# The first unit's x and f_logit loaded by rows and transposed on TensorE, with two more edits at the start of a float32 scan and two-MLP kernel

## The chip, the core and the metric

One Trainium2 chip, one of its cores. The metric is the device time of one execution in microseconds (us); lower is better. The engines are TensorE (PE; PEld is its weight load), VectorE (DVE), ScalarE (ACT), GpSimd (POOL) and SyncE (SP), whose queue issues nearly all transfers.

## The reference

`x` and `f_logit` are (2, 6080, 256), the weights are drawn as float64 and used as two int32 words each (low, high).

```
sig = 1 / (1 + exp(-f_logit)); f = lower_bound + (1 - lower_bound) * sig
h = f[:, t] * h + (1 - f[:, t]) * x[:, t]; y[:, t] = h      # gated scan over t, from h = 0
z = square(relu(y @ w_in1)) @ w_out1                        # 256 -> 2048 -> 256, 12160 tokens
out = elu(z @ w_in2) @ w_out2                               # 256 -> 2048 -> 256
```

## The kernel before

The 12160 tokens are cut into 12 units: the first has two halves of 512 and 384 tokens, all others two halves of 512. Everything on the chip is held with the model dimension on the partitions, as two blocks of 128 (index `c`), and tokens along the row. Float32 products are made of three fp32r matmuls (high by high, high by low, low by high), so each weight and each activation is split into a high part (a copy on ACT or DVE) and a low part (a subtraction on DVE).

The scan is made in four chunks a unit (two for each half). For a chunk `add_scan` issues: loads of f_logit (`fs`) and x (`xs`) on SP, in four transfers each; tanh on ACT (L573); two DVE transposes, `xT` and `fT` (L578; 32 by 32 blocks); for the first chunk the bounds `ga`, `gb` (L588, L589); two gates (L584); the feed `xT = (fT - 1) * xT` (L592); two scans, one for each block `c` (L605); and a copy of the last column to `carry` (L610). A half's parts `xa` or `xb` follow: high on ACT (L485), low on DVE (L488).

The first two units of the first MLP are "plain": for a group `g` of 256 hidden units the PE makes two PSUM tiles (`c0`, `c1`, then `c2`, `c3`) of six matmuls each (L636), ACT takes relu (L728) and square (L661) and the high part `g` (L676), DVE the low part (L681), and the PE then adds `g` by the output weights `wo` into `a00` to `a11` (L858). Units from the third on, and the whole second MLP, use a form with seven weight sums and fewer matmuls.

Weights are prepared on the chip while the first units run: a load `st` (L316 for `w_in1`, L308 for `w_out1`), two ACT steps (L372 for the magnitude, L375 for the low bits), two DVE steps (L378, L381), then the high part on ACT (L407) and the low part on DVE (L413). The first of them is loaded by ACT's queue, the others by SP's. There are three `st` buffers.

The order on each engine is made once, ahead of the run, by `Order.run`: a list scheduler with planned costs (`act(n)`, `dve(n)`, `ROW` us for each column of a matmul) that takes on each engine the ready step with the earliest due time. On the chip each engine then works its list in that order and waits at each instruction for what it needs. DVE and ACT therefore hold up all that stands behind a waiting instruction. A step with an alternative (`("ACT", ...)`) goes to the engine that the planner finds free first.

Of the kernel before, what the change touches and what calls it, by code (L numbers as in the profile page):

```python
# [6 lines left out]

F32 = mybir.dt.float32
# [15 lines left out]
ROW = 1 / 2240  # L24
# [4 lines left out]
    "fs": 2, "xs": 2, "fT": 1, "xT": 1, "F0": 1, "F1": 1, "xa": 1, "xb": 1, "ws": 2, "wp": 2, "r": 3, "e": 2,  # L29
# [122 lines left out]
def kernel(  # L152
# [31 lines left out]
    warm = const.tile([P, 1], F32, name="warm")  # L184
    const.tile([P, GAP], F32, name="gap")
# [20 lines left out]
    def plain(m, u):  # L206
        return m == 0 and u < PLAIN

    def halves(m, u):
        return units[u] if plain(m, u) else (sum(units[u]) // 2,) * 2  # L210
# [85 lines left out]
    def key_of(tag):  # L296
        count[tag] = count.get(tag, -1) + 1
        return tag, count[tag]
# [5 lines left out]
    def load_w(queue, st, m, kind, c):  # L304
        w = ((w_in1, w_out1), (w_in2, w_out2))[m][kind].bitcast(I32)
        if kind == 1:
            v = w[c * CF : (c + 1) * CF, :].rearrange("(k p) u -> p k u", p=P)
            queue.dma_start(st.rearrange("p k e w -> p k (e w)"), v)  # L308
        elif m == 1:
            v = w[:, 2 * c * CF : 2 * (c + 1) * CF].rearrange("(k p) u -> p k u", p=P)  # L310
            queue.dma_start(st.rearrange("p k e w -> p k (e w)"), v)
        else:

            v = w[:, 2 * c * CF : 2 * (c + 1) * CF].rearrange("(q k i) u -> q i k u", q=4, k=KD)
            for q in range(4):
                queue.dma_start(st[32 * q : 32 * q + 32].rearrange("p k e w -> p k (e w)"), v[q])  # L316
# [37 lines left out]
    def add_weights(i, m, kind, c, due, wk=None):  # L354
        t = {}

        def load(e):
            t["st"] = new("st", [P, 2, CE // 2, 2], I32)
            if i == 0:
                nc.scalar.activation(warm, warm, AF.Exp)  # L360
            load_w(nc.scalar if i == 0 else nc.sync, t["st"], m, kind, c)
            if i == 0:
                for k in range(KD):
                    nc.scalar.dma_start(lb[:, k : k + 1], lower_bound.rearrange("(q c i o) -> c q i o", q=4, c=KD, o=1)[k])
            sv = t["st"].rearrange("p k e w -> p (k e) w")
            t["low"], t["high"] = sv[:, :, 0], sv[:, :, 1]
# [51 lines left out]
        def keep_whole(e):  # L418
# [4 lines left out]
            ["ACT" if i == 0 else "SP", 5.8 if i == 0 else 1.9 if m == 0 and kind == 0 else 0.475, load, (), [st], None, 512],  # L423
# [5 lines left out]
        if i == 0:  # L429
            steps[0][4].append(("lb",))  # L430
            order.add(*steps[0][:2], -20.0, *steps[0][2:])
            del steps[0]
# [58 lines left out]

    def add_parts(m, u, F, due, later):

        ns = halves(m, u)
        if plain(m, u):
            for h, n in enumerate(ns):
                tag = ("xa", "xb")[h]
                k = key_of(tag)
                x_k[m, u, h] = [(*k, 0), (*k, 1)]
                def dst(h=h, tag=tag, n=n):  # L500
                    if (m, u, h) not in x_t:
                        x_t[m, u, h] = new(tag, [P, 2, 3 + h, HN], F32R)[:, :, :2, :n]
                    return x_t[m, u, h]
                def src(h=h, n=n):
                    return F_t[m, u][:, h : h + 3 : 2, :n]
                high, low = split(src, dst)
                chain(in_due[m, u, h, 0], [
                    ["ACT", act(2 * n), high, F[h], [x_k[m, u, h][0]]],
                    ["DVE", dve(2 * n), low, [x_k[m, u, h][0], *F[h]], [x_k[m, u, h][1]]],
                ])  # L510
            return
        n = ns[0]
# [43 lines left out]

    def add_scan(i, u, h, q, due, after=None):
        nh = units[u][h]
        n = nh // 2
        t0 = starts[u] + sum(units[u][:h]) + q * n  # L560
        at = q * n
        t = {}

        def load(x, src):
            def go(e):
                t[x] = new(x, [P, CN // 32, KD, 32])[:, : n // 32]
                v = src[t0 : t0 + n, :].rearrange("(n j) (q u) -> q j n u", j=32, q=4)
                for q in range(4):
                    nc.sync.dma_start(t[x][32 * q : 32 * q + 32].rearrange("j n c i -> j n (c i)"), v[q])  # L569
            return go  # L570
# [3 lines left out]

        def turn(src, dst):
            def go(e):
                t[dst] = new(dst, [P, KD, CN])[:, :, :n]
                nc.vector.transpose(t[dst].rearrange("p c (n i) -> p n c i", i=32), t[src])  # L578
            return go
# [29 lines left out]
        def carry_on(e):  # L609
# [5 lines left out]
        opened = [("F0", u, 0, 0)] * (h + q > 0)  # L615
        chain(due, [
# [5 lines left out]
            *([["DVE", 0.2, bound, [("lb",)], [("bound",)]]] if i == 0 else []),  # L622
            *(["DVE", dve(n, True), gate(c), [("bound",)], [fT]] for c in range(KD)),
            ["DVE", dve(N), feed, [fT], [xT]],
            *(["DVE", dve(n) + 0.1, scan(c), [fT, xT, ("carry",), *opened], [F]] for c in range(KD)),
# [80 lines left out]
    def add_plain(s, wk):  # L706
# [24 lines left out]
        for c in range(2):  # L731
            k = order.add("PE", 6 * ROW * n, in_due[s] + 6 * c * ROW * n, product(c), [*x_k[m, u, h], wk], [ck[c], ("pe",)])
            if c == 0:
                n_first[s] = k
# [227 lines left out]
    n_scan = 0  # L962
    for kind, s in pe_order:
        if kind == "out":
            add_out(s)
            continue
        m, u, h, g = s
        if kind != "later" and s == first_of[m, u]:
            if m == 0:
                keys = {}  # L970
                before = slots_of(0, u - 1)
                for hh in range(2):
                    due = in_due[(m, u, hh, 0) if plain(m, u) else s]
                    for q in range(2):
                        k = before[SCANS[2 * hh + q] * len(before) // KG] if u >= BEHIND else None
                        keys[hh, q] = add_scan(n_scan, u, hh, q, due - 6.0 + 2.0 * (q - 1), n_first[k] if k else None)
                        n_scan += 1
                if plain(m, u):
                    add_parts(m, u, [[keys[hh, 0], keys[hh, 1]] for hh in range(2)], None, None)
                else:  # L980
                    f0, f1 = ([keys[hh, 0], keys[hh, 1]] for hh in range(2))
                    add_parts(m, u, (f0, f0, f1, f1), in_due[s], mid_due[s])
            else:
                add_parts(m, u, add_reload(u, in_due[s]), in_due[s], mid_due[s])
        if kind == "plain":
            add_plain(s, use[s])
        elif kind == "first":
            add_first(s, use[s])
        else:
            add_later(s)  # L990

    with tc.manual_schedule():
        nc.vector.memset(warm, 0.0)
        order.run()
# [25 lines left out]
```

## Time and profile before

| | |
|---|---|
| time of the runs | 2000.31 us median (2000.08, 2000.31, 2001.04) |
| profiled execution | 2000.24 us, span of the trace 1998.4 us |
| PE busy | 1963.1 us (98%) |
| DVE busy | 1674.6 us (84%) |
| ACT busy | 1633.3 us (82%) |
| first matmul starts | 19.61 us |

The execution's own time is 1.84 us more than the span of its trace. A matmul of 512 columns takes 0.227 us where twelve run back to back at full clock (2.72 us for twelve). An engine's column "idle before" names what ended the wait. "SPq" and "ACTq" are transfers being issued by those engines.

### The profile page before, as it was taken

The page shows a single profiled execution, that of the slowest core. Times are in us where ns is not written, and L with a number is a line of the kernel's source. Part 1 is how long each engine was busy: PE and PEld are TensorE (multiplying, and loading weights), DVE is VectorE, ACT ScalarE, POOL GpSimd, SP SyncE. Part 2 cuts the span into 40 slices and gives each one's busy share as a digit, 9 for nine tenths or more (in the row PEclk, how much of TensorE's full clock was granted, in tenths as well). Part 3 has the DMA queues.
Part 4 walks back from the last instruction along what each step waited for, and adds up shares of the span by engine and source line. Part 5 has one row for each costly group of instructions (what it writes and reads, how often), then busy time and mean ns, then how long its engine had stood idle before and what let it go on. Part 6 is the DMA issues. An engine that isn't in the chain of part 4 may idle for free.

```text
span 1998.4 us, 24516 instructions
## 1 busy us (share of the span) xinstructions
PE 1963.1 (98%) x8688; PEld 1628.9 (82%) x8688; DVE 1674.6 (84%) x2291; ACT 1633.3 (82%) x2164; POOL 0.2 (0%) x4
## 2 busy tenths in 40 slices
PE   5999999999999999999999999999999999999998
PEld 4987888888888888888888888888888888888886
DVE  7879998887987987888898798798888887779886
ACT  6988988888888888878888888887887888788885
POOL 0000000000000000000000000000000000000000
PEclk9999999999999999999999999999999999999999
DMA  7877762433443344244243344334324323334231
GB/s 196 244 226 229 263 207 93 143 129 108 125 127 113 126 122 134 96 148 139 86 136 122 113 135 127 121 111 137 129 83 132 134 93 113 114 113 135 87 106 53
DMA packets 235138, 267.30 MB, mean 134 GB/s; under 512 B 160008, under 2 KB 160776, under 8 KB 235016
## 3 DMA queue, kind: packets, MB, share of 16 engines
q1 hardware_dynamic: 234432, 265.21, 41.6%
q8 instruction: 68, 1.11, 0.2%
q10 hardware_dynamic: 584, 0.53, 0.1%
q14 instruction: 54, 0.44, 0.1%
HBM read 221.91 MB, written 43.78 MB: 133 GB/s over the span
## 4 chain that ended last, share of the span: by engine, by line
PE 91%; DVE 5%; DMA 1%; ACT 1%; issue 1%; SPq 1%; DVEq 0%; ACTq 0%
PE a L858 48%; PE c L636 43%; DVE g L681 1%; DVE a L342 1%; SPq L569 0%; DMA fs<-in_f_logit_dram 0%; DMA a<-rd 0%; DMA xs<-in_x_dram 0%; ACT g L676 0%; DMA st<-in_moe_w_in_dram 0%; DVE a L378 0%; DVE a L381 0%; DVE fT L578 0%; DVE F L605 0%; DVE s L763 0%
## 5 line engine op out<-in xcount | busy, mean ns | idle before, releaser
L858 PE MATMUL a<-g,wo 128*128 128x512 f32 (+1 forms) x4608 | 1099.0, 387 | 1.2 <-DVE g L681 1.0
L858 PEld LDWEIGHTS a<-g,wo 128*128 128x128 f32 x4608 | 863.3, 188 | 175.5 <-DVE g L681 3.1
L681 DVE TENSOR_TENSOR g<-r,g 128x1024 fp32r<-128x1024 f32 (+2 forms) x384 | 463.0, 1206 | 153.6 <-ACT g L676 152.0
L636 PE MATMUL c<-xb,ws 128*128 128x512 f32 (+2 forms) x2208 | 525.9, 387 | 0.0
L636 PEld LDWEIGHTS c<-xb,ws 128*128 128x128 f32 x2208 | 414.0, 188 | 82.4
L676 ACT ACTIVATE g<-r 128x1024 fp32r<-128x1024 f32 (+2 forms) x384 | 403.6, 1051 | 94.1 <-PE a L858 82.8
L636 PE MATMUL c<-xa,ws 128*128 128x512 f32 (+1 forms) x1680 | 417.7, 392 | 27.1 <-ACT xa L485 19.6
L636 PEld LDWEIGHTS c<-xa,ws 128*128 128x128 f32 x1680 | 316.4, 189 | 98.2 <-ACT xa L485 19.6
L759 ACT ACTIVATE s<-c 128x512 f32<-128x512 f32 (+1 forms) x528 | 307.5, 588 | 14.1 <-PE c L636 13.5
L671 DVE SCALAR_TENSOR_TENSOR r<-e,r 128x1024 f32<-128x1024 f32 (+1 forms) x192 | 232.1, 1209 | 29.9 <-ACT e L668 29.9
L665 ACT ACTIVATE e<-r 128x1024 f32<-128x1024 f32 (+1 forms) x192 | 201.7, 1051 | 48.7 <-DVE r L803 48.3
L661 ACT ACTIVATE r<-r 128x1024 f32<-128x1024 f32 x192 | 201.8, 1051 | 2.4
L668 ACT ACTIVATE e<-e 128x1024 f32<-128x1024 f32 (+1 forms) x192 | 201.7, 1050 | 1.6
L763 DVE TENSOR_TENSOR s<-s 128x512 f32<-128x512 f32 (+1 forms) x176 | 119.9, 681 | 74.5 <-ACT s L759 74.5
L799 ACT ACTIVATE r<-c 128x512 f32<-128x512 f32 (+1 forms) x176 | 104.2, 592 | 82.6 <-PE c L636 82.1
L796 DVE TENSOR_TENSOR s<-c,s 128x512 f32<-128x512 f32 (+1 forms) x176 | 120.3, 684 | 20.3 <-PE c L636 18.0
L807 DVE TENSOR_TENSOR r<-c,s 128x512 f32<-128x512 f32 (+1 forms) x176 | 119.3, 678 | 4.5 <-DVE g L681 0.5
L803 DVE TENSOR_TENSOR r<-c,s 128x512 f32<-128x512 f32 (+1 forms) x176 | 119.6, 680 | 2.1
L810 DVE TENSOR_TENSOR r<-s 128x512 f32<-128x512 f32 (+1 forms) x176 | 119.1, 677 | 0.0
L655 ACT ACTIVATE r<-r 128x1024 f32<-128x1024 f32 x80 | 84.4, 1055 | 3.3 <-DVE r L810 3.3
L658 ACT ACTIVATE r<-r 128x512 f32<-128x512 f32 x80 | 50.4, 630 | 33.7 <-DVE r L803 33.0
L605 DVE TENSOR_TENSOR_SCAN F<-fT,carry,xT 128x256 f32<-128x256 f32 (+2 forms) x94 | 65.4, 723 | 1.1
(47 smaller groups left out, 757.2 us busy)
## 6 DMA issues: line engine op xcount, KB each, us to landing
ws<-wd SPq DMA_DIRECT2D x176, 896.0 KB, 4.9
fs<-in_f_logit_dram SPq DMA_DIRECT2D x184, 64.0 KB, 2.2
xs<-in_x_dram SPq DMA_DIRECT2D x184, 64.0 KB, 2.2
xd<-o SPq DMA_DIRECT2D x46, 256.0 KB, 4.5
F<-xd SPq DMA_DIRECT2D x22, 512.0 KB, 4.5
out_dram<-o SPq DMA_DIRECT2D x88, 128.0 KB, 2.3
st<-in_moe_w_out_dram SPq DMA_DIRECT2D x16, 512.0 KB, 5.2
wd<-wp SPq DMA_DIRECT2D x24, 256.0 KB, 3.7
```

The source lines that it names most:

```text
L636: nc.tensor.matmul(out, lhsT=ws[:, p, w], rhs=xs[:, r, v], start=start and q == 0, stop=stop and q == 2, skip_group_check=check,)
L661: nc.scalar.activation(r_t[0], r_t[0], AF.Square)
L665: nc.scalar.activation(t["e"], r_t[0], AF.Relu, scale=-1.0)
L668: nc.scalar.activation(t["e"], t["e"], AF.Exp, scale=-1.0)
L671: nc.vector.scalar_tensor_tensor(r_t[0], t["e"], 1.0, r_t[0], op0=ALU.subtract, op1=ALU.max)
L676: nc.scalar.activation(g_t[s, which][:, 0], r_t[0], AF.Copy)
L681: nc.vector.tensor_tensor(g_t[s, which][:, 1], r_t[0], g_t[s, which][:, 0].bitcast(F32), op=ALU.subtract)
L759: nc.scalar.activation(t["s"][:, c - 1], t[c], AF.Copy)
L763: nc.vector.tensor_tensor(t["s"][:, 1], t["s"][:, 1], t["s"][:, 2], op=ALU.add)
L796: nc.vector.tensor_tensor(t["s"][:, 0], t[0], t["s"][:, 0], op=ALU.add)
L803: nc.vector.tensor_tensor(odd[0][:, 1], t[2], t["s"][:, 0], op=ALU.add)
L858: nc.tensor.matmul(a, lhsT=y, rhs=v, start=begin and jj == 0 and p == 0, stop=end and jj == len(mine) - 1 and p == 2, skip_group_check=True,)
```

## The change

Five things are edited.

1. `w_in1`'s rows and all scan channels are paired: partition p holds model dimensions 2p and 2p + 1 rather than one from each of two 32-blocks. A load of `w_in1` and of `lower_bound` is then one transfer each instead of four and two, and the DVE transposes of later units read their source at a step of two elements.
2. For the first unit `fs` and `xs` are loaded by rows (tokens on the partitions, one transfer each), and the PE transposes them into PSUM against an identity `one`; tanh and the feed read PSUM. The identity is made on GpSimd by `make_identity`. The unit's chunks are cut at multiples of 128 tokens: 256, 256, 256 and 128 (before: 256, 256, 192, 192).
3. The first half's parts are made for each block `c` apart, high and low, and the first group's products are ordered by block: six matmuls that need only block 0, then six for block 1.
4. `fT` has two buffers; the second half's scans are entered in the order after the first half's.
5. The planner's costs: `ROW` from 1/2240 to 1/2258, a gate at `dve(n)`, a scan at `0.1 + n / 490`, one load of `w_in1` at 0.475.

```diff
-ROW = 1 / 2240
+ROW = 1 / 2258
-    ... "fT": 1, ...
+    ... "fT": 2, ...
@@ load_w
-            v = w[:, 2 * c * CF : 2 * (c + 1) * CF].rearrange("(q k i) u -> q i k u", q=4, k=KD)
-            for q in range(4):
-                queue.dma_start(st[32 * q : 32 * q + 32].rearrange("p k e w -> p k (e w)"), v[q])
+            v = w[:, 2 * c * CF : 2 * (c + 1) * CF].rearrange("(p k) u -> p k u", k=KD)
+            queue.dma_start(st.rearrange("p k e w -> p k (e w)"), v)
+    def add_first_parts(F, k, src, dst, n, due):
+        x_k[0, 0, 0] = [(*k, c, p) for c in range(KD) for p in range(2)]
+        cut = [split(lambda c=c: src()[:, c], lambda c=c: dst()[:, :, c]) for c in range(KD)]
+        for c, (high, low) in enumerate(cut):
+            f = [(*v, c) for v in F]
+            hi, lo = (*k, c, 0), (*k, c, 1)
+            order.add("ACT", act(n), due - 3.0, high, f + [(*k, 0, 0)] * c, [hi])
+            order.add("DVE", dve(n), due - 2.0, low, [hi, *f], [lo])
@@ add_scan
+        def load_rows(x, src):
+            def go(e):
+                t[x] = new(x, [P, CN // 32, 32, KD]).rearrange("p n i c -> p (n i c)")[:, : n * KD].rearrange("p (k d) -> p k d", d=D)
+                nc.sync.dma_start(t[x], src[t0 : t0 + n, :].rearrange("(k p) d -> p k d", p=P))
+            return go
+        def turn_rows(x, tag):
+            def go(e):
+                out = pools[tag].tile([P, HN], F32, tag=tag, name=tag)
+                t[tag] = out.rearrange("p (c n) -> p c n", c=KD)[:, :, :n]
+                v = t[x].rearrange("p k (i c) -> p k c i", c=KD)
+                for k in range(n // P):
+                    for c in range(KD):
+                        nc.tensor.transpose(t[tag][:, c, k * P : (k + 1) * P], v[:, k, c], one)
+            return go
-                nc.vector.transpose(t[dst].rearrange("p c (n i) -> p n c i", i=32), t[src])
+                nc.vector.transpose(t[dst].rearrange("p c (n i) -> p n c i", i=32), t[src].rearrange("p n i c -> p n c i"))
+        if u == 0:
+            tags = [("c0", "c1"), ("c2", "c3"), ("a10", "a11"), ("a00", "a01")][i]
+            pf, px = (key_of(tag) for tag in tags)
+            order.add("SP", 0.6, -20.0 + 2 * i, load_rows("fs", ff), (), [fs], None, n)
+            order.add("SP", 0.6, -19.0 + 2 * i, load_rows("xs", xf), (), [xs], None, n)
+            if i == 0:
+                order.add("SP", 0.6, -18.5, load_bound, (), [("lb",)])
+            order.add("PE", 0.1 * n / P * KD, due - 6.0, turn_rows("fs", tags[0]), [fs, ("one",)], [pf, ("pe",)])
+            order.add("PE", 0.1 * n / P * KD, due - 6.0, turn_rows("xs", tags[1]), [xs], [px, ("pe",)])
+            chain(due, [
+                ["ACT", act(N, True), tanh_turned(tags[0]), [pf], [fT]],
+                *([["DVE", 0.2, bound, [("lb",)], [("bound",)]]] if i == 0 else []),
+                *(["DVE", dve(n), gate(c), [("bound",)], [fT]] for c in range(KD)),
+                ["DVE", dve(N), feed_turned(tags[1]), [px, fT], [xT]],
+                *(["DVE", 0.1 + n / 490, scan(c), [fT, xT, ("carry",), *opened], [F, (*F, c)]] for c in range(KD)),
+                ["DVE", 0.1, carry_on, [F], [("carry",)]],
+            ])
+            return F
@@ add_plain
+        if n_plain[0] == 1:
+            for k in range(2):
+                x_k1 = x_k[m, u, h][2 * k : 2 * k + 2]
+                n1 = order.add("PE", 6 * ROW * n, in_due[s] + 6 * k * ROW * n, products_of(k), [*x_k1, wk], [ck[0], ck[1], ("pe",)])
@@ end
         nc.vector.memset(warm, 0.0)
+        make_identity(nc, one)
         order.run()
```

On the PE the list of matmuls is otherwise the same from end to end; what is new stands at its start. Before, the first rows of PE are these (`xa` is the first half's parts, `ws` and `s` are weights):

```order
L636 MATMUL c0_290<-xa_272,ws_249 128x512 x6
L636 MATMUL c1_305<-xa_272,ws_249 128x512 x6
L636 MATMUL c2_334<-xa_272,s_317 128x512 x6
L636 MATMUL c3_348<-xa_272,s_317 128x512 x6
L636 MATMUL c0_374<-xa_272,ws_365 128x512 x6
```

With the change PE begins with transposes of the chunks (L595; `fs` and `xs` are the rows loaded, `one` the identity):

```order
L595 MATMUL c0_206<-one_63,fs_193 128x128 x4
L595 MATMUL c1_216<-one_63,xs_195 128x128 x4
L595 MATMUL c2_227<-one_63,fs_198 128x128 x4
L595 MATMUL c3_238<-one_63,xs_200 128x128 x4
L595 MATMUL a10_264<-one_63,fs_214 128x128 x4
L595 MATMUL a11_273<-one_63,xs_225 128x128 x4
L702 MATMUL c0_289<-xa_281,ws_243 128x512 x3
L702 MATMUL c1_293<-xa_281,ws_243 128x512 x3
L702 MATMUL c0_289<-xa_281,ws_243 128x512 x3
L702 MATMUL c1_293<-xa_281,ws_243 128x512 x3
L595 MATMUL a00_319<-one_63,fs_236 128x128 x2
L595 MATMUL a01_324<-one_63,xs_256 128x128 x2
```

Three chunks are transposed ahead of the first product; the fourth chunk's transposes stand behind the first group's twelve matmuls.

On DVE the first rows before are these, from the first chunk's transposes to the second's (`a`, `st` and `ws` belong to the first weights):

```order
L578 STREAM_TRANSPOSE xT_214<-xs_198 128x8x2x32
L578 STREAM_TRANSPOSE fT_216<-fs_193 128x8x2x32
L588 TENSOR_SCALAR ga_59<-lb_58 128x2
L589 TENSOR_SCALAR gb_60<-lb_58 128x2
L584 TENSOR_SCALAR fT_216<-fT_216,ga_59,gb_60 128x256 x2
L592 SCALAR_TENSOR_TENSOR xT_214<-fT_216,xT_214 128x512
L605 SCALAR_TENSOR_TENSOR F0_237<-fT_216,xT_214 128x256
L378 SCALAR_TENSOR_TENSOR a_227<-a_227,st_185 128x512
L605 SCALAR_TENSOR_TENSOR F0_237<-fT_216,xT_214 128x256
L381 SCALAR_TENSOR_TENSOR a_227<-st_185,a_227 128x512
L578 STREAM_TRANSPOSE xT_247<-xs_208 128x8x2x32
L578 STREAM_TRANSPOSE fT_251<-fs_203 128x8x2x32
```

With the change these rows stand behind the first gate (L633, of `fT_212`), which itself stands behind the first weights' magnitude (L375); the last row is the second chunk's scan of block 0:

```order
L378 SCALAR_TENSOR_TENSOR a_204<-st_190,a_204 128x512
L633 TENSOR_SCALAR fT_212<-fT_212,ga_59,gb_60 128x256
L618 SCALAR_TENSOR_TENSOR xT_245<-fT_212,c1_216 128x512
L633 TENSOR_SCALAR fT_233<-fT_233,ga_59,gb_60 128x256
L654 SCALAR_TENSOR_TENSOR F0_250<-fT_212,xT_245 128x256
L633 TENSOR_SCALAR fT_233<-fT_233,ga_59,gb_60 128x256
L654 SCALAR_TENSOR_TENSOR F0_250<-fT_212,xT_245 128x256
L410 TENSOR_TENSOR ws_243<-a_204,ws_243 128x512
L618 SCALAR_TENSOR_TENSOR xT_262<-fT_233,c3_238 128x512
L659 COPY carry_61<-F0_250 128x2
L375 SCALAR_TENSOR_TENSOR a_254<-a_254,st_202 128x512
L654 SCALAR_TENSOR_TENSOR F0_250<-fT_233,carry_61,xT_262 128x256
```

The four transposes of the two chunks are gone from DVE. GpSimd, which had only four small memsets to do, now makes the identity, with an instruction that the list names only ISA between its two steps:

```order
L1105 MEMSET const-float32-0.0 128x1
L1105 MEMSET const-float32-1.0 128x1
L1105 MEMSET const-bfloat16-1.0 128x1
L1105 MEMSET const-uint8-127 128x1
L1115 UNCONDITIONAL_BRANCH
masks.py:197 MEMSET one_63 128x128
masks.py:199 ISA
masks.py:199 AFFINE_SELECT one_63<-one_63 128x128
```

The first transpose on PE waits for the last of these rows and for the first chunk's `fs`.

## Rows read from the trace of the kernel before

**Rows 1.** What the PE waited for, whole span: total us, times, longest.

```profile
PE c L636 <- ACT xa L485: 19.6, 1, 19.6
PE c L636 <- ACT ws L407: 2.7, 1, 2.7
PE c L636 <- ACT r L728: 2.3, 1, 2.3
```

**Rows 2.** Busy time by stretch: us, PE, PEld, DVE, ACT, POOL, PEclk, DMA share, GB/s.

```profile
34.00:36.00 2.00, 2.00 (x6) 1.52 (x6) 1.80 (x4) 1.97 (x4) 0.00 (x0) 0.50 1.03 388
...
150.00:310.00 160.00, 156.22 (x695) 129.47 (x694) 156.63 (x268) 139.69 (x209) 0.00 (x0) 1.00 0.70 224
...
500.00:1000.00 500.00, 500.00 (x2203) 413.06 (x2202) 424.13 (x562) 413.68 (x535) 0.00 (x0) 1.00 0.38 122
```

**Rows 3.** Timeline to the first matmul: start, us, engine, line, operation, count, idle before.

```profile
0.80 0.06 DVE L993 MEMSET warm<- 128x1 f32 x1 [0.80 <-PEq L1006]
0.90 1.35 ACTq L316 DMA_DIRECT2D st<-in_moe_w_in_dram  x3
...
6.18 0.63 ACT L573 ACTIVATE fs<-fs 128x512 f32<-128x512 f32 x1 [3.95 <-DMA lb<-in_lower_bound_dram]
...
8.28 0.71 DVE L578 STREAM_TRANSPOSE xT<-xs 128x512 f32<-128x512 f32 x1 [7.42 <-DMA xs<-in_x_dram]
...
10.51 0.69 DVE L592 SCALAR_TENSOR_TENSOR xT<-fT,xT 128x512 f32<-128x512 f32 x1
10.59 0.65 ACT L372 ACTIVATE a<-st 128x512 f32<-128x512 f32 x1
11.15 0.66 ACT L375 ACTIVATE st<-st 128x512 int32<-128x512 uint32 x1
11.23 0.69 DVE L605 TENSOR_TENSOR_SCAN F<-fT,xT 128x256 f32<-128x256 f32 x1
11.84 0.69 DVE L378 SCALAR_TENSOR_TENSOR a<-a,st 128x512 int32<-128x512 int32 x1
12.45 0.68 DVE L605 TENSOR_TENSOR_SCAN F<-fT,xT 128x256 f32<-128x256 f32 x1
...
14.86 0.12 DVE L610 COPY carry<-F 128x2 f32<-128x2 f32 x1
14.97 0.41 DVE L584 TENSOR_SCALAR fT<-fT,ga,gb 128x256 f32<-128x256 f32 x1
15.30 0.68 DVE L413 TENSOR_TENSOR ws<-a,ws 128x512 fp32r<-128x512 f32 x1
...
17.07 1.39 DVE L605 TENSOR_TENSOR_SCAN F<-fT,carry,xT 128x256 f32<-128x256 f32 x2
18.50 1.06 ACT L485 ACTIVATE xa<-F 128x1024 fp32r<-128x1024 f32 x1 [1.66 <-DVE F L605]
```

**Rows 4.** Timeline of PE alone from its first matmul to the first outputs.

```profile
19.61 0.79 PE L636 MATMUL c<-xa,ws 128*128 128x512 f32 x1 [19.61 <-ACT xa L485]
21.32 4.88 PE L636 MATMUL c<-xa,ws 128*128 128x512 f32 x11 [0.92 <-DVE xa L488]
26.04 2.93 PE L636 MATMUL c<-xa,s 128*128 128x512 f32 x12
31.70 4.87 PE L636 MATMUL c<-xa,ws 128*128 128x512 f32 x12 [2.73 <-ACT ws L407]
36.41 2.27 PE L636 MATMUL c<-xb,ws 128*128 128x384 f32 x12
...
41.27 2.88 PE L858 MATMUL a<-g,wo 128*128 128x512 f32 x12
```

**Rows 5.** Transfers of the first 60 us: issues, KB each, median us to landing.

```profile
st<-in_moe_w_out_dram SPq DMA_DIRECT2D x5, 512.0 KB, 5.3
...
wd<-ws SPq DMA_DIRECT2D x3, 512.0 KB, 7.1
...
fs<-in_f_logit_dram SPq DMA_DIRECT2D x8, 64.0 KB, 2.0
```

## What is predicted

> **What bounds the kernel now.** The page first: PE is the bound, and from 300 us on it is busy without a gap; the stretch 500 to 1000 us shows 500.00 of 500.00 [rows 2]. There the change has nothing to win, for the matmuls and their order stay the same. So I read what PE waits for. Of 35.3 us in which it is not busy (1998.4 less 1963.1), 19.6 are one wait, for the first half's high part `xa` on ACT; 2.7 are a wait for the third weights `ws`; 2.3 one for a relu [rows 1]. Then the timeline of the opening. ACT's tanh waits 3.95 us and starts at 6.18, DVE starts its first transpose at 8.28 after 7.42 idle, and from there DVE is the path: both scans of two chunks, mixed with the first weights, end at 18.46; `xa` takes 1.06 and PE starts at 19.61 [rows 3, 4]. After that PE is not yet at full pace: from 19.61 to the first outputs at 41.27 are 21.66 us, in which lie 48 matmuls of 512 columns (4 x 2.72) and twelve of 384 (36.41 to the next group at 38.52: 2.11), 12.99 us of work at full clock [rows 4]. 8.67 us are lost there: waits of 0.92 and 2.73, and slow matmuls. The second and the fourth row of the group take 4.88 for eleven and 4.87 for twelve, 0.44 and 0.41 each against 0.227. In the latter the granted clock reads 0.50, the 1.2 GHz level [rows 2], and PE had stood idle for 2.73 us before it.
>
> So what can be won are the 19.6 us and the 8.7 behind them.
>
> **The opening with the change: the identity.** PE's first transpose needs rows of `fs` and the identity. The rows come early: one transfer issued near 0.8, landing some 2.0 us after issue [rows 5], so near 3.2. The identity is made by GpSimd: a memset, the ISA instruction, a select. The engines leave the opening at 0.80 [rows 3]. No row has any of the three. The memset I put at 0.2, the select at no more than a 512-column DVE operation, 0.7. What the ISA instruction does no row says. From below it costs nothing; from above I take the slowest thing an engine can wait for in the opening, a transfer of 7.1 us [rows 5]. If it is a small step, the identity is ready before the rows; if it fetches something from memory, it does so beside some 2 MB of loads. I take the upper end, since an instruction that the builder puts there for one select alone must set something up, and a fetch is what it is nearest to: 0.8 + 0.2 + 7.1 + 0.7 = 8.8 us.
>
> The Trainium skill, GPSIMD Engine Reference, section 2.1 (Instruction dispatch), says that the first call of a freshly loaded GpSimd kernel pays a code load of about 6 us (5.95 measured) that shows as no instruction in a profile. By it the identity would be ready at 7.65 and the sum below would come to 1994.5. No run here shows it yet.
>
> **From the identity to the first matmul.** Four transposes make the first `fs` tile. A 128-column transpose is between a quarter of a slow 512-column matmul (0.11) and the whole of it (0.44) [rows 4]; I take 0.2, so 0.8. Tanh takes 0.63 [rows 3], with three hand-overs of 0.05. The first gate then starts at G = identity + 1.6 = 10.4. ACT's list has the first weights' two steps ahead of the tanh; their load, issued at 0.90, lands by 6.2 to 6.6 (5.3 for 512 KB [rows 5]), and they end by 7.8, so they are covered, with the first weights' magnitude on DVE. If the identity were early, they would set G: 6.2 + 0.56 + 0.66 + 0.63, near 8.05.
>
> Behind the first gate DVE works the rows shown for the change. From start to start a gate takes 0.33 (14.97 to 15.30), a scan or a 512-column operation 0.61 (11.23, 11.84, 12.45), the copy 0.11 (14.86 to 14.97), and one that needs the result just before it 0.7 (10.51 to 11.23) [rows 3]. So: gates 4 x 0.33, sign, low part, magnitude 3 x 0.60, feeds 0.65 + 0.60, two scans 1.22, copy 0.11, and the last scan to its end 0.69, in all 6.4. Then the high part of block 0 on ACT, 0.63, and two hand-overs: PE starts at G + 7.25 = 17.65, not 19.61. That is 1.96 us. The four DVE transposes that are gone (8 with the other chunks) would be worth more, but DVE now starts two us later than 8.28.
>
> **From the first matmul to the first outputs.** The same walk along the three lists, in us from G. Matmul 1 at 7.25, the second waits for block 0's low part until 8.08 (loss 0.6). Eleven at 0.44 last until 12.92 (loss 2.35), as they did before: PE has done only 24 short transposes or waited. The fourth chunk's transposes behind them cost 0.58. Here is the new wait: ACT's fourth tanh needs those transposes, so ACT stands from 11.6 to 13.2 and DVE, which has that chunk's gates next, until 13.65; behind them is the second weights' low part, ready at 14.85, for which PE waits 0.95. After that ACT (relu, square, high part) and DVE are ahead of PE by little: 0.08 at the third weights' low part, 0.28 at `xb`, and 0.35 and 0.69 where `c0` and `c1` are freed by a relu. The outputs start at 26.15: 18.9 us after the first matmul, 5.9 of them lost, where 8.67 were. That is 2.76 more. The largest part is that the 2.73 wait for the third weights and the slow twelve behind it go, since no idle of that length is left; `st` loads are one transfer each and in SP's list sooner.
>
> **Costed at nothing.** The later units' DVE transposes read at a step of two. L378 reads `st` at such a step and takes 0.69, L592 reads in a row and takes 0.69 [rows 3]; so nothing, and from 300 us on DVE has 76 of 500 us to cover it [rows 2]. The new costs of gate and scan and `ROW` move rows on DVE and ACT all along. Where PE has no gap that changes nothing. In 150 to 310 us DVE is busy for 156.63 of 160 and PE loses 3.8 [rows 2]: there a new order can win those 3.8 or lose as much again; I take 0. What starts earlier shifts this stretch as a whole, since what DVE waits for comes from PE and ACT. The first unit's transfers: SP issues 1 where there were 4, off the path. SP's third `fs` load waits for the first transposes (buffers), lands near identity + 3.3, needed at G + 6: covered by 4 us. The split high part costs ACT 0.2, in idle time.
>
> **Sum.** 1.96 + 2.76 = 4.7 us. 2000.24 - 4.7 = 1995.5; the profiled execution is 0.07 under the median, so 1995.6 for the median. In one formula: gain = 13.5 - identity.
>
> **Rivals.**
> 1. *The identity is early* (ISA costs next to nothing). G is 8.05, PE starts at 15.3; 4.3 + 2.8 = 7.1: 1993.2. For it: GpSimd has nothing else to do. Against it: the instruction is there. Transposes at 0.11 belong here, too.
> 2. *The identity is later still*, 9.5 to 13.5: the gain is 4 to 0, 1996.3 to 2000.3, no change by 0.2% (4.0 us, about what a measurement of this kernel tells from none). Transposes at 0.44 add 1.0 on this side. For it: at 2 to 10 us the DMA engines carry the first loads, which any fetch competes with. Against it: nothing in the opening takes longer than 7.1.
> 3. *The gain is given back where DVE is full.* If in 150 to 310 us DVE waits for loads, not for PE and ACT, it can't start sooner, and PE waits 4.7 more: 2000.3. For it: 156.63 of 160. Against it: over the span DVE is busy for 84%, so it has room to run ahead elsewhere.
> 4. *Slower: the new DVE order in that stretch.* A low part `g` set behind other work costs PE a stall as the 2.3 us for a relu [rows 1]. Two more such stalls eat the gain; from four on (9.2 - 4.7 = 4.5 lost) the kernel is slower by 0.2%: 2004.8. For it: the planner's DVE costs changed there. Against it: the new costs (0.33 and 0.62) are those that the trace shows (0.33, 0.61), and PE's order is unchanged.
>
> **Chances.** The forecast (identity 7.5 to 9.5) 0.45, with its own range of 1993.8 to 1997.5; rival 1 0.18; rival 2 0.19; rival 3 0.10; rival 4 0.08. Faster by over 0.2% takes rival 1 and some four fifths of the forecast: 0.54; slower rival 4: 0.08; the rest, 0.38, within. The range from 1992 (rival 1, with a stall fewer in 150 to 310) to 2000 leaves out rival 4 and an edge of rivals 1 and 3.
>
> **What would show it.** POOL's select ending near 8.8, and PE's first transpose just behind it; the first gate 1.6 later; a first product near 17.6 and the first outputs near 36.6; no granted 0.50 near 30 us; ACT and DVE idle some 1.5 us before the fourth tanh; 150 to 310 us with a PE idle of about 3.8. Wrong would be: an identity beyond 13.5, transposes slower than 0.44 each, or new gaps of PE behind 100 us.

## The result and the profile after

The changed kernel takes **1981.62 us** (median of 4 runs, 1981.28 to 1982.57) beside 2000.19 for the kernel before: ratio 0.9909, 95% interval 0.9892 to 0.9927. It is faster by 18.6 us, four times the 4.7 predicted, and outside the range. The profiled execution took 1981.58 us, with a span of 1979.8.

What PE waited for over the whole span, to read against [rows 1] (total us, times, longest):

```profile
PE c L595 <- DMA fs<-in_f_logit_dram: 3.7, 1, 3.7
PE c L702 <- ACT xa L481: 3.2, 1, 3.2
PE c L595 <- DMA xs<-in_x_dram: 1.8, 1, 1.8
PE c L702 <- DVE s L410: 1.1, 1, 1.1
...
PE c L702 <- ACT r L794: 0.3, 1, 0.3
PE a L938 <- DVE g L747: 0.3, 1, 0.3
```

The wait of 19.6 us for `xa` is now 3.2, with 3.7 and 1.8 for the rows to be transposed ahead of it. The wait for the third weights is gone (the 1.1 is for the second), and the 2.3 us for a relu are 0.3. GpSimd is nowhere in this list.

Busy time by stretch, with the columns of [rows 2]:

```profile
34.00:36.00 2.00, 2.00 (x11) 1.65 (x10) 1.16 (x2) 2.00 (x6) 0.00 (x0) 1.00 0.92 351
150.00:310.00 160.00, 160.00 (x730) 136.71 (x729) 154.92 (x257) 145.63 (x218) 0.00 (x0) 1.00 0.66 215
500.00:1000.00 500.00, 500.00 (x2207) 413.75 (x2206) 425.76 (x566) 412.44 (x531) 0.00 (x0) 1.00 0.39 123
```

From 150 to 310 us PE is busy for all 160.00; before it was 156.22.

The timeline to the first matmul, beside [rows 3]:

```profile
0.73 0.20 POOL masks.py:197 MEMSET one<- 128x128 f32 x1 [0.29 <-POOLq L1105]
0.74 0.45 SPq L585 DMA_DIRECT2D fs<-in_f_logit_dram  x1
...
1.01 0.29 POOL masks.py:199 TENSOR_SCALAR_AFFINE_SELECT one<-one 128x128 f32<-128x128 f32 x1
...
3.65 1.10 PE L595 MATMUL c<-one,fs 128*128 128x128 f32 x4 [3.65 <-DMA fs<-in_f_logit_dram]
...
6.13 0.67 ACT L369 ACTIVATE a<-st 128x512 f32<-128x512 f32 x1 [3.90 <-DMA st<-in_moe_w_in_dram]
...
6.70 0.66 ACT L372 ACTIVATE st<-st 128x512 int32<-128x512 uint32 x1
...
7.25 0.59 ACT L612 ACTIVATE fT<-c 128x512 f32<-128x512 f32 x1
...
8.00 0.41 DVE L633 TENSOR_SCALAR fT<-fT,ga,gb 128x256 f32<-128x256 f32 x1
...
14.51 0.63 ACT L481 ACTIVATE xa<-F 128x512 fp32r<-128x512 f32 x1 [1.83 <-DVE F L654]
...
20.48 0.39 ACT L612 ACTIVATE fT<-a 128x256 f32<-128x256 f32 x1 [1.03 <-PE a L595]
...
20.90 0.35 DVE L633 TENSOR_SCALAR fT<-fT,ga,gb 128x128 f32<-128x128 f32 x1 [0.77 <-ACT fT L612]
```

GpSimd's select starts 0.08 us after its memset ends, and the identity is ready at 1.30. PE's first transpose waits for the rows of `fs`. The first tanh stands on ACT behind the two steps of the first weights, which wait for their load until 6.13.

PE alone from its first product to the first outputs, beside [rows 4]:

```profile
15.19 4.96 PE L702 MATMUL c<-xa,ws 128*128 128x512 f32 x12 [3.24 <-ACT xa L481]
19.99 0.39 PE L595 MATMUL a<-one,fs 128*128 128x128 f32 x2
...
22.23 2.57 PE L702 MATMUL c<-xa,s 128*128 128x512 f32 x10 [1.14 <-DVE s L410]
24.63 3.06 PE L702 MATMUL c<-xa,ws 128*128 128x512 f32 x12
...
33.22 2.88 PE L938 MATMUL a<-g,wo 128*128 128x512 f32 x12
```

**Where the 18.6 us come in.** Both traces have the same 8688 products in the same order (but for the first twelve, ordered by block after), so the start of the k-th product before, less its start after, is the lead of the change at that point. Read at a few products:

| product | start before, us | lead, us |
|---|---|---|
| 1st | 19.6 | 4.4 |
| 61st, the first outputs | 41.3 | 8.1 |
| 601st | 155.8 | 9.2 |
| 721st | 183.6 | 9.8 |
| 781st | 200.4 | 13.0 |
| 1381st | 332.9 | 15.4 |
| 7981st | 1829.2 | 17.3 |
| 8688th, the last | 1991.0 | 18.0 |

Two parts, then: about 9 us that are there by 156 us, nearly all from the opening, and about 9 more behind it, 6.2 of them between 156 and 333 us.

**A place of the second part.** Before, ACT's and DVE's timeline around 185 us reads:

```profile
183.14 1.04 ACT L676 ACTIVATE g<-r 128x1024 fp32r<-128x1024 f32 x1
...
184.22 1.23 DVE L681 TENSOR_TENSOR g<-r,g 128x1024 fp32r<-128x1024 f32 x1 [1.72 <-ACT g L676]
...
185.17 1.04 ACT L485 ACTIVATE xb<-F 128x1024 fp32r<-128x1024 f32 x1
...
186.11 0.57 ACT L728 ACTIVATE r<-c 128x512 f32<-128x512 f32 x1
```

and PE's beside it:

```profile
183.64 0.84 PE L636 MATMUL c<-xa,ws 128*128 128x512 f32 x3
186.74 2.02 PE L636 MATMUL c<-xa,ws 128*128 128x512 f32 x6 [2.26 <-ACT r L728]
```

This is the 2.3 us of [rows 1]. PE waits for a relu that frees a tile `c`. The relu stands in ACT's list behind `xb`, but that is the smaller part of it: it also needs one of the three `r` buffers, the one that the group three before it gives back when its low part (the row of L681) has read it. That low part waits 1.72 us for its `g` on ACT and ends at 185.45, so with another place in ACT's list the relu could have started 0.66 us sooner at most. At the same products after, the low part (L747) ends at 172.42, ahead of the products at 173.82 and not 1.81 behind those at 183.64, and PE goes through:

```profile
170.11 1.04 ACT L742 ACTIVATE g<-r 128x1024 fp32r<-128x1024 f32 x1
...
171.19 1.23 DVE L747 TENSOR_TENSOR g<-r,g 128x1024 fp32r<-128x1024 f32 x1 [0.46 <-ACT g L742]
...
172.51 0.60 ACT L794 ACTIVATE r<-c 128x512 f32<-128x512 f32 x1 [0.23 <-DVE g L747]
...
173.82 2.20 PE L702 MATMUL c<-xa,ws 128*128 128x512 f32 x9
```

One step of the difference is that ACT's list before has `xa` (176.94) ahead of the `g` of the group before (177.89), and the list after has it behind (164.97 for `g`, 165.92 for `xa`). The rest lies further back and was not followed. This place is worth 2.9 of the 6.2 us (the lead is 9.8 at 183.6 us and 12.7 at 188.6). Two more of the rises, 0.8 near 270 us and 1.0 near 300, are where PE waited before for a sum on DVE that frees a tile (L807, 0.49 and 0.72 us).

### The profile page after: what moved, and what is told of

The parts are those of the page before. It is cut to its first block, busy times and chain, and to the rows that moved or that the text cites. A ratio compares the mean times of both kernels' runs of the same rounds, so it can differ in the third digit from the quotient of the medians.

```text
span 1979.8 us, 24508 instructions
## 1 busy us (share of the span) xinstructions
PE 1962.0 (99%) x8716; PEld 1633.2 (82%) x8716; DVE 1673.0 (85%) x2292; ACT 1631.8 (82%) x2157; POOL 0.7 (0%) x6
## 4 chain that ended last, share of the span: by engine, by line
PE 98%; ACT 1%; DVE 1%; DMA 0%; issue 0%; DVEq 0%; ACTq 0%
PE a L938 52%; PE c L702 46%; DMA st<-in_moe_w_in_dram 0%; ACT g L742 0%; ACT r L794 0%; DVE F L654 0%; DVE g L747 0%; ACT r L727 0%; ACT xb L481 0%; ACT st L372 0%; DVE fT L633 0%; DVE o L978 0%; DVE xT L618 0%; ACT a L369 0%; DVE r L737 0%
## 5 line engine op out<-in xcount | busy, mean ns | idle before, releaser
L747 DVE TENSOR_TENSOR g<-r,g 128x1024 fp32r<-128x1024 f32 (+2 forms) x384 | 464.3, 1209 | 129.9 <-ACT g L742 129.5
L702 PE MATMUL c<-xa,ws 128*128 128x512 f32 (+1 forms) x1680 | 411.7, 390 | 3.7 <-ACT xa L481 3.2
L839 ACT ACTIVATE s<-c 128x512 f32<-128x512 f32 (+1 forms) x528 | 306.9, 587 | 14.2 <-PE c L702 13.5
L887 DVE TENSOR_TENSOR r<-c,s 128x512 f32<-128x512 f32 (+1 forms) x176 | 119.8, 681 | 3.5 <-PE a L938 0.5
```

The source lines that it names most:

```text
L702: nc.tensor.matmul(out, lhsT=ws[:, p, w], rhs=xs[:, r, v], start=start and q == 0, stop=stop and q == 2, skip_group_check=check,)
L747: nc.vector.tensor_tensor(g_t[s, which][:, 1], r_t[0], g_t[s, which][:, 0].bitcast(F32), op=ALU.subtract)
L839: nc.scalar.activation(t["s"][:, c - 1], t[c], AF.Copy)
```

## The experiments

"Changed" below is the kernel after; each lead is read as in the table, from one trace of each version. The kernel before was run anew beside each set of runs, with medians of 1999.66 to 2000.86 us, so a difference of about 1 us between versions of different sets tells nothing.

**The opening or the planner's costs.** Three runs part the change: the kernel before with the new costs alone, the kernel before with the pairing alone, and the changed kernel with the old costs.

```diff
-ROW = 1 / 2240
+ROW = 1 / 2258
-            *(["DVE", dve(n, True), gate(c), ...
+            *(["DVE", dve(n), gate(c), ...
-            *(["DVE", dve(n) + 0.1, scan(c), ...
+            *(["DVE", 0.1 + n / 490, scan(c), ...
```

> The kernel before with the planner's new costs alone (ROW 1/2258, gate dve(n), scan 0.1 + n/490). Theory P (the planner's costs remove the later stalls): the first matmul stays near 19.6 us, but the lead over the kernel before grows by 7 to 10 us between 150 and 340 us, time near 1990. Theory L (the later gain comes with the earlier start or with the fewer transfers): no lead, 1998 to 2002.

Pairing alone in the kernel before:

```diff
-            for q in range(4):
-                queue.dma_start(st[32 * q : 32 * q + 32]..., v[q])
+            queue.dma_start(st.rearrange("p k e w -> p k (e w)"), v)
-                nc.vector.transpose(t[dst]..., t[src])
+                nc.vector.transpose(t[dst]..., t[src].rearrange("p n i c -> p n c i"))
...
```

(With it go one transfer for `lower_bound` and the planned cost of a `w_in1` load, 0.475, and 1.6 for the first.)

> The kernel before with the paired model dimension alone: w_in1 and lower_bound in one transfer each, later DVE transposes at a step of two, the planner's cost of that load. Theory S (fewer transfers in SP's list bring the weights sooner): first matmul up to 2 us sooner, the third weights' wait of 2.7 us gone, 5 to 12 us faster in all. Theory P: within 3 us of before. If a step of two slowed the DVE transposes, they would take over 0.75 us.

The changed kernel with the costs of the first diff undone:

> The changed kernel with the planner's old costs (ROW 1/2240, gate and scan as before). Theory P: opening as in the changed kernel (first matmul 15.2, outputs 33.2), then 5 to 10 us lost again by 340 us, time 1987 to 1992. Theory L or S: within 2 us of 1981.6.

Measured: the costs alone 1991.98 us (0.9962, 0.9947 to 0.9976); the pairing alone 1999.80 (0.9999, 0.9990 to 1.0009); the changed kernel with old costs 1991.14 (0.9956, 0.9940 to 0.9971). Beside the 2000.07 of the kernel before in this set, the opening edits alone are worth 8.9 us and the costs alone 8.1, which make 17.0 of the 18.6; each is worth more on top of the other (10.4 and 9.5). The costs alone lose 0.6 by the first outputs and have a lead of 0.7 at 183.6 us, 3.8 at 200.4, 5.9 at 332.9 and 8.7 at the end. With the old costs the lead is 8.3 at the first outputs and 8.8 at the end. From 150 to 310 us, the costs alone in the kernel before:

```profile
150.00:310.00 160.00, 159.94 (x724) 135.34 (x723) 156.22 (x264) 143.68 (x214) 0.00 (x0) 1.00 0.70 221
```

So the gain behind the opening is the list that the new costs make, and DVE is as full there as before (156.22 beside 156.63 [rows 2]). The step of two in DVE's transposes and the single transfers change nothing in the whole time; the list made with them has PE wait 3.98 us for the second weights and loses 2.6 us by the first outputs, of which 1.1 are left at the end.

**Which of the costs.** The first diff's first line alone, and its other two alone, in the kernel before.

> The kernel before with ROW 1/2258 alone. If the pace that the planner gives PE is what matters, the 8 us of the cost edits are here (near 1992). If the costs of gate and scan on DVE are what matters, within 2 us of 2000.

> The kernel before with the costs of gate and scan alone (0.33 for 0.20, 0.62 for 0.43). If a DVE that was planned too fast is what made PE wait between 150 and 340 us, most of the 8 us are here (1992 to 1994) and PE's idle time of 3.8 us in 150 to 310 falls below 1. If the pace of PE is what matters, within 2 us of 2000.

Measured: `ROW` alone 1995.88 (0.9979, 0.9969 to 0.9988), the costs of gate and scan alone 1999.91 (0.9999, 0.9989 to 1.0008). Together they gave 8.1, so the effects of the two don't add.

**How the first unit is transposed.** The changed kernel with the first unit on the later units' path (DVE transposes, no identity):

```diff
-        if u == 0:
+        if False:
...
+            *(... "SP", 0.6, load_bound, ... "DVE", 0.2, bound, ... if i == 0 else []),
...
-        make_identity(nc, one)
```

> The changed kernel with the first unit's x and f_logit loaded and transposed by DVE as before (no identity, no PE transposes); all else as changed. Theory P: it loses the opening's 4 to 8 us but keeps the later gain, 1986 to 1990. Theory L (the earlier start is what removes the later stalls): it loses nearly all, 1996 to 2000.

Measured: 1989.32 us (0.9947, 0.9931 to 0.9963). The first product starts at 19.75, as before, and the lead at the first outputs is 1.74 where the changed kernel's is 8.05. Of the change's 18.6 us, 7.7 need the transposes on PE, most of them (6.3) in the opening.

**A late identity.** The identity is delayed by 27 more memsets on GpSimd, to the time that was forecast.

```diff
+        for _ in range(27):
+            nc.gpsimd.memset(one, 0.0)
         make_identity(nc, one)
```

> The changed kernel with 27 more memsets on GpSimd ahead of the identity, so that it is ready near 8.5 to 9 us as the prediction took it. If the walk of the opening is right: first matmul near 17.7, first outputs near 36 (a lead of about 5 over before), and the later gain as in the changed kernel, 1984 to 1985 in all. If the opening has slack for the identity, 1981 to 1982.

Measured: 1984.73 us (0.9921, 0.9905 to 0.9938). Its timeline:

```profile
0.73 7.03 POOL L1093 MEMSET one<- 128x128 f32 x27 [0.29 <-POOLq L1107]
...
8.10 0.29 POOL masks.py:199 TENSOR_SCALAR_AFFINE_SELECT one<-one 128x128 f32<-128x128 f32 x1
...
8.45 1.12 PE L595 MATMUL c<-one,fs 128*128 128x128 f32 x4 [8.45 <-POOL one masks.py:199]
...
10.24 0.41 DVE L633 TENSOR_SCALAR fT<-fT,ga,gb 128x256 f32<-128x256 f32 x1 [2.51 <-ACT fT L612]
...
17.44 0.79 PE L702 MATMUL c<-xa,ws 128*128 128x512 f32 x1 [3.28 <-ACT xa L481]
```

The identity is ready at 8.39, where 8.8 had been taken; the first gate follows at 10.24, the first product at 17.44, and the first outputs at 36.62. The forecast of this case was 10.4, 17.65 and 36.6. The lead at the first outputs is 4.66, where the formula (13.5 less 8.39) gives 5.1. It is 3.4 less than in the changed kernel, and the whole time is 3.1 longer: what the opening wins arrives at the end.

**What bounds the opening now.** First, `lower_bound` goes ahead of `fs` on SP, and the first load's planned cost is raised so that the tanh stands ahead of the first weights on ACT:

```diff
-            ["ACT" if i == 0 else "SP", 1.0 if i == 0 else 0.475, load, ...
+            ["ACT" if i == 0 else "SP", 3.5 if i == 0 else 0.475, load, ...
-                order.add("SP", 0.6, -18.5, load_bound, (), [("lb",)])
+                order.add("SP", 0.6, -20.5, load_bound, (), [("lb",)])
```

> The changed kernel with the planner's cost of the first weights' load at 3.5 (it was 1.0; the load was seen to land at 6.1) and lower_bound loaded first: the first tanh then stands ahead of the first weights on ACT. If the first gate waits for ACT's weight steps, it starts near 5.6 and the first matmul 1 to 2 us sooner than 15.2: 1979.5 to 1981. If the x rows, landing at 6.5, set the chain, no gain: 1981 to 1982.5.

Measured: 1987.59 us (0.9938, 0.9923 to 0.9953), 6.0 slower than the changed kernel: 2.8 of it by the first outputs, the rest behind them, where its lists are others. `fs` is issued only 0.46 us later, but behind ACT's load of 512 KB:

```profile
0.91 0.67 ACTq L316 DMA_DIRECT2D st<-in_moe_w_in_dram  x1
1.20 0.41 SPq L585 DMA_DIRECT2D fs<-in_f_logit_dram  x1
...
6.27 1.10 PE L595 MATMUL c<-one,fs 128*128 128x128 f32 x4 [6.27 <-DMA fs<-in_f_logit_dram]
...
8.04 0.74 DVE L633 TENSOR_SCALAR fT<-fT,ga,gb 128x256 f32<-128x256 f32 x2 [5.29 <-ACT fT L612]
```

PE can use it only 2.6 us later, and the first gate starts at 8.04, no sooner. From 2.3 to 3.4 us all packets moved are of ACT's queue. `lower_bound` is ahead of `fs` too, on its own queue; its packets are over by 2.3 us, and what share of the delay it has no run parts. Then the same wish without that fault: `lower_bound` on ACT's queue, so that `fs` and `xs` both leave early; the first load's planned cost stays at 3.5.

```diff
+            if i == 0:
+                nc.scalar.dma_start(lb, lower_bound.rearrange("(i c) -> i c", c=KD))
...
-        chain(due, [
+        chain(due - 8.0 if i == 0 else due, [
...
-                order.add("SP", 0.6, -18.5, load_bound, (), [("lb",)])
```

> The changed kernel with lower_bound on ACT's queue ahead of the first weights, so that these are issued behind the rows of x, and with the first tanh ahead of the weights on ACT. If transfers land in the order of issue, x lands near 4.5 (6.5 before), the first gate starts near 5.5 (8.0), the first matmul near 13.2 (15.2); 2 us sooner at the first outputs. If the planner's lists behind it keep the later gain, 1979 to 1980; if they change as they did with the tanh first, 1981 to 1986.

Measured: 1983.53 us (0.9912, 0.9898 to 0.9927). The tanh starts at 4.93, not 7.25, but the first weights land later, as ACT's timeline shows:

```profile
4.93 0.60 ACT L614 ACTIVATE fT<-c 128x512 f32<-128x512 f32 x1 [2.70 <-PE c L597]
7.81 0.68 ACT L371 ACTIVATE a<-st 128x512 f32<-128x512 f32 x1 [2.29 <-DMA st<-in_moe_w_in_dram]
```

PE waits 2.30 us for the second `fs`, and the first product starts at 15.31 beside 15.19. In these two orders, whichever load goes first, the other is late. That points to the opening being bound by its transfers together, but no run with fewer transfers shows it.

**Two smaller parts.** The first half's parts and products whole again, not by block:

```diff
-        if u == 0 and h == 0:
+        if False:
-        if n_plain[0] == 1:
+        if False:
```

> The changed kernel with the first half's parts made whole and the first group's products ordered as before. By the walk of the prediction the high part waits for the second chunk's second scan and takes 1.06 for 0.63: first matmul 1.2 to 1.5 us later (16.5), outputs about 1 later; the later gain as in the changed kernel, 1982 to 1983.5.

One buffer for `fT` instead of two:

```diff
-    "fT": 2, ...
+    "fT": 1, ...
```

> The changed kernel with one buffer of fT. The tanh of the second chunk then waits for the first chunk's scans and the second chunk's gates come later: first matmul 0.5 to 1.5 us later; if the second buffer also helps later units, 1 to 3 us more between 150 and 340 us. 1982 to 1986.

Measured: whole parts 1983.46 us (0.9913, 0.9896 to 0.9930), the first product 1.0 later, 1.8 in all. One `fT` 1990.89 (0.9949, 0.9934 to 0.9964): 2.5 of its 9.3 us are gone by the first outputs, the rest behind them, where PE waits 4.2 for relus and is busy for 156.40 of 160 from 150 to 310 us. One buffer also makes the planner another list, and this run doesn't part the buffer from the list.

**Are the new costs better because they are true?** A `ROW` of 1/2258 is the pace that PE keeps: 12 x 512 / 2258 is 2.72 us, as read before. If that is why the list got better, the time should rise smoothly with the distance from it. Six other values, each the one change:

```diff
-ROW = 1 / 2258
+ROW = 1 / 2250
```

> The changed kernel with ROW 1/2240 alone. With the kernel before, ROW alone gave 4.4 us, the costs of gate and scan alone nothing, both 8.7. If both are needed for the later gain, this one loses 7 to 9.5 us, as with all old costs (1989 to 1991); if the two only add, 4 to 5 us (1986). The gain of 0.4 us a unit behind 500 us is gone in either case.

> The changed kernel with the planner's cost of a matmul column at 1/2250 instead of 1/2258, nothing else. Theory (the later gain is there because the planner's cost now is the pace that TensorE really keeps): the pace is 0.35% off, so the time lies between the changed kernel's 1981.6 and the 1987.7 of the run with the old 1/2240: about 1984, with most of the loss as a creep of the lead after 333 us. Rival (the lists of 150 to 333 us came out well by chance, and any other value deals them anew): the time scatters with no order, 1980 to 1989, and may be below the changed kernel's.

> The changed kernel with the planner's cost of a matmul column at 1/2270, as far beyond the measured pace as the old 1/2240 is short of it. Theory (true cost): slower than 1981.6, by 1 to 4 us. Rival (chance): anywhere from 1980 to 1989; a time below 1981 speaks for it.

> The changed kernel with the planner's cost of a matmul column at 1/2290. Theory (true cost): slower than the run at 1/2270, 1983 to 1990. Rival (chance): no order between this run, the one at 1/2270 and the one at 1/2250.

> The changed kernel with the planner's cost of a matmul column at 1/2256 instead of 1/2258, 0.09% off. So small an error of the cost is worth nothing by itself. Theory (true cost): within 1 us of 1981.6. Rival (each value deals a new list, and the lists differ by luck): 1980 to 1992, with a fair chance of 3 us or more off 1981.6.

> The changed kernel with the planner's cost of a matmul column at 1/2261 instead of 1/2258, 0.13% off to the other side. Theory (true cost): within 1 us of 1981.6. Rival (each value deals a new list): 1980 to 1992, with a fair chance of 3 us or more off 1981.6.

| 1 / ROW | time, us | ratio, interval | lead at first outputs | lead won 156 to 333 us | lead won 333 us to the last product |
|---|---|---|---|---|---|
| 2240 | 1987.68 | 0.9936, 0.9921 to 0.9951 | 7.4 | 3.9 | -0.3 |
| 2250 | 1991.84 | 0.9957, 0.9942 to 0.9972 | 7.4 | -0.1 | 0.5 |
| 2256 | 1987.32 | 0.9934, 0.9920 to 0.9949 | 8.1 | 1.0 | 2.8 |
| 2258 | 1981.62 | 0.9909, 0.9892 to 0.9927 | 8.1 | 6.2 | 2.6 |
| 2261 | 1984.35 | 0.9922, 0.9906 to 0.9939 | 8.1 | 4.4 | 2.0 |
| 2270 | 1983.97 | 0.9918, 0.9903 to 0.9933 | 7.4 | 4.5 | 1.6 |
| 2290 | 2002.57 | 1.0009, 0.9999 to 1.0019 | 7.9 | 5.0 | -17.2 |

The opening hardly moves, but what follows does not follow the distance. A value 0.09% off (2256) costs 5.7 us, one 0.13% off (2261) 2.7; 2250 is nearer than 2240 and 4.2 slower. (The intervals of 2240, 2256, 2261 and 2270 overlap that of 2258, though their four runs each, 1983.31 us at the least, all lie above its four, 1982.57 at the most; 2250 and 2290 are clear of it.) So each value makes a list of its own. The run at 2256 has the trouble of the kernel before at the same products again; its ACT list puts `xb` (L481) and weights ahead of the second relu:

```profile
176.68 0.60 ACT L794 ACTIVATE r<-c 128x512 f32<-128x512 f32 x1
177.16 0.70 ACT L372 ACTIVATE st<-st 128x512 int32<-128x512 uint32 x1
177.73 1.06 ACT L481 ACTIVATE xb<-F 128x1024 fp32r<-128x1024 f32 x1
178.68 0.60 ACT L794 ACTIVATE r<-c 128x512 f32<-128x512 f32 x1
```

and PE waits at both:

```profile
177.34 0.98 PE L702 MATMUL c<-xa,ws 128*128 128x512 f32 x3 [1.86 <-ACT r L794]
179.33 1.36 PE L702 MATMUL c<-xa,ws 128*128 128x512 f32 x3 [1.02 <-ACT r L794]
```

At 2290 the damage is elsewhere. Its DVE list puts two steps of 1.22 us ahead of the sum that frees the third `c` tile (L887):

```profile
660.32 1.22 DVE L747 TENSOR_TENSOR g<-r,g 128x1024 fp32r<-128x1024 f32 x1
661.46 1.22 DVE L737 SCALAR_TENSOR_TENSOR r<-e,r 128x1024 f32<-128x1024 f32 x1
662.60 0.68 DVE L887 TENSOR_TENSOR r<-c,s 128x512 f32<-128x512 f32 x1
```

and PE waits in every round of the list, nine times between 333 and 1829 us, some 165 us apart:

```profile
498.23 0.96 PE L702 MATMUL c<-xa,ws 128*128 128x512 f32 x3 [1.61 <-DVE r L887]
663.33 0.96 PE L702 MATMUL c<-xa,ws 128*128 128x512 f32 x3 [1.61 <-DVE r L887]
```

The lead shrinks by 1.67 at each, 15.0 in all, about what it had won by 333 us. The small creep of the changed kernel's lead (1.9 us from 333 to 1829) is the same thing with the other sign: 1.7 of it come in nine steps of 0.19 at these same products.

Last, the planned cost of a scan, so that DVE counts as slower than it is:

```diff
-... 0.1 + n / 490, scan(c) ...
+... 0.1 + n / 420, scan(c) ...
```

> The changed kernel with the planner's cost of a scan at 0.1 + n/420 instead of 0.1 + n/490, so that VectorE counts as slower than it is. Theory (true cost): the stretch from 150 to 310 us loses some of its 160.00 us of TensorE work again, 1 to 6 us slower than 1981.6. Rival (chance): no change or a gain as likely as a loss.

Measured: 1982.29 us (0.9910, 0.9895 to 0.9924), 0.7 from the changed kernel, which can't be told from none. That cost matters little once the rest is as it is.

No version tried beat the changed kernel; the nearest were this one, the whole parts and the rows first.

## Why the prediction was too small

Of the 13.9 us that the forecast fell short, 3.4 had come in by the first outputs and the rest behind them.

**The identity was mis-sized.** The ISA instruction between memset and select was taken at its upper bound, 7.1 us. The trace has 0.08 between them, and at that line only two steps of GpSimd's queue, MODIFY_POOL_CONFIG, of 0.01 each. The reasons given for the upper end (it must set something up, and a fetch is the nearest thing) were an analogy, not a row. The Trainium skill, GPSIMD Engine Reference, section 2.1 (Instruction dispatch), speaks of a code load of about 6 us at a freshly loaded kernel's first call; the trace shows no such time here. What came is rival 1's opening: first gate at 8.00 (8.05), first product at 15.19 (15.3), a lead of 8.1 at the first outputs (7.1).

**The walk was right.** From the first gate to the first product it was 7.19 us (7.25 forecast, though the addends with hand-overs of 0.05 give 7.13), to the first outputs 25.2 (26.15). From the gate at 10.24 in the late-identity run it was 7.20 and 26.4. The new wait is where it was named: ACT idle for 1.03 before the fourth tanh (20.48; some 1.6 forecast), DVE for 0.77 before its gate, PE for 1.14 before the second weights' low part (0.95). No 0.50 stands in the clock between 34 and 36 us. The 0.95 that the second walk was long lies in the first products: from the second of them to the fourth chunk's transposes 3.91 us (16.08 to 19.99) passed, not 4.84 (11 x 0.44), because they quicken after the eighth. In the late-identity run they don't: from the first product to those transposes it takes 5.75 us (17.44 to 23.19), in the changed kernel 4.80.

**A transfer was mis-sized without harm.** `fs` in one transfer of 256 KB takes 4.9 us to land, not the 2.0 of a 64 KB one in [rows 5]. PE's third transposes waited 0.62 for it (9.97), but ACT came to that tanh at 12.08, later for another reason.

**The costs taken at nothing were worth 8 to 9.5.** "there a new order can win those 3.8 or lose as much again; I take 0" is the step that failed most. The place of gain and loss was named rightly, and its bound was too tight: PE lost 3.8 us inside 150 to 310 us, but slower products and the stretch up to 333 us belonged to it too, so 6.2 was won there. That from 500 us on there was nothing to win was too strong also, since a lead of 0.19 a round adds up without a gap that a busy share shows. Rivals 3 and 4 did not come: PE is busy for 160.00 of 160 with DVE at 154.92. Rival 4's mechanism, a low part `g` behind other work, is real all the same. It worked the other way: the kernel before had it at 186.74 us, and the new lists took it away. The run at 2290 loses 17 us by its like, a sum on DVE that frees a tile too late. The second `fT` buffer is in no term of the sum; without it 9.3 of the 18.6 us are gone, by the buffer or by the list that goes with it.

**What stays open.** That 1/2258 is the best of seven values is measured; why is not. That it is the true pace is no sufficient reason, as 1/2256 shows. At the places read here PE waits where steps of ACT and DVE stand ahead of those that free a tile or a buffer, and each value deals that anew. No pattern in the lists was found that would have told the seven apart ahead of the runs.

## What to carry to other kernels

Don't cost a change of a list scheduler's numbers at nothing because the bound engine's own list stays the same: look in the new lists of the other engines, which are fixed ahead of the run, for steps that stand ahead of one that frees a tile, or a buffer that this one needs. If such numbers are cheap to vary, run several; one value's result is a draw (here 1981.6 to 2002.6), and the rest of a change is then read at a point ahead of where the lists differ, by the lead at matched instructions. An instruction that no row shows should keep both bounds until something is measured, and in an opening look at what is issued ahead of a small early load: here 0.46 us later became 2.6.

## What the runs showed of the hardware

A 256 KB load issued at 0.74 us, ahead of a 512 KB load on another queue, was used at 3.65; issued at 1.20 behind it (and behind 1 KB on its own queue), at 6.27: 0.46 later became 2.6 later. On GpSimd a memset of 128 by 128 takes 0.20 us (27 in a row 7.03), the select 0.29, and between them lie 0.08 us. Four float32 transposes of 128 by 128 take 1.10 us. DVE's transposes at a step of two take 709 and 674 ns in the median, beside 703 and 669. And PE's pace at the start of the products is not all in the granted clock: the column reads 1.00 from 16.60 to 18.80 us, where these seven start 0.43 us or more apart:

```profile
16.08 3.16 PE L702 MATMUL c<-xa,ws 128*128 128x512 f32 x7
```

In the late-identity run the column reads 0.50, the 1.2 GHz level, from 17 to 20 us, and the first products there are 0.43 apart too; ahead of its first product PE had waited 3.28 us there, and 3.24 in the changed kernel. What sets the pace where the column reads 1.00 was not tried further.
